# Pooled attention and a feed-forward layer on one core: half of the first loads issued by ScalarE, and a quarter of h copied out of its bank before g is made from it

## Chip, cores and metric

The kernel runs on one core of a Trainium2 chip. The metric is the device time of one execution in microseconds (us). Before the change three runs took 940.62, 941.49 and 943.90 us, so the median is 941.49 us. One further execution was recorded by the hardware profiler; it took 947.1 us.

## The reference

Keys and values are averaged over groups of 8 positions, so each of 8 batches and 8 heads has 576 queries but only 72 keys. The attention's result is laid out as 4608 tokens of 512 numbers and goes through a feed-forward layer of width 2048.

```python
batch, n_heads, seq, head_dim = (8, 8, 576, 64)
k_p = k.reshape(B, H, Sp, 8, D).mean(axis=3)
v_p = v.reshape(B, H, Sp, 8, D).mean(axis=3)
scores = scale * np.matmul(q, k_p.transpose(0, 1, 3, 2))
scores = scores - np.max(scores, axis=-1, keepdims=True)
attn = np.exp(scores)
attn = attn / (np.sum(attn, axis=-1, keepdims=True) + 1e-09)
attn_out = np.matmul(attn, v_p)
x = attn_out.transpose(0, 2, 1, 3).reshape(B * S, H * D)   # 4608 x 512
h = x @ w_in                                               # 512 x 2048
g = h * (1.0 / (1.0 + np.exp(-1.702 * h)))
out = g @ w_out                                            # 2048 x 512
```

## The kernel before

**Work.** All numbers are fp32. Every matrix operand of the feed-forward layer is kept as a rounded high part and a rest, and a product is three matmuls (high by high, rest by high, high by rest). Tokens go in chunks of 512. Chunk c is the first 512 tokens of batch c; chunk 8 gathers the 64 tokens that are left over in each batch. Chunks 0 and 1 are done by `dense`. While chunk 0 runs, the weights are still being loaded and decoded (`fetch_weights`, `decode`). From chunk 2 on, h is made pair by pair (`pair`): pair p of a chunk is two blocks of 128 columns of h by two halves of 256 tokens, that is four quarters, and these four quarters come from seven products instead of eight, with sums of weights that `fold` has stored in DRAM (`wd`) and that `fetch_pair` loads again for each chunk (`ws`, and `shared` for the fourth, half-sized part). During a chunk's eight pairs, the attention of the next batch is worked in between (`sum_keys`, `scores`, `sum_values`, `weigh`). The output products of pair p (`outputs`, tiles `o`) are placed among the products of pair p+1.

**A pair.** Two PSUM banks, `ha` and `hb`, hold running sums; all pairs and the dense chunks together have two buffers of this kind, so the next pair's `ha` is the last pair's `ha` buffer again, and its first product waits until that is read to the end. Four products go to `ha` (by the names of the weights: 11, s2, s3, 22), three to `hb` (12, s1, s4). After the first three products into `ha` the running sum is copied to a place in SBUF (`keep`, L1442); sums from `hb` are added to these places (`plus`, L1449). From a place, ScalarE makes g twice (`gelu`: L1466 the rounded high part `ghall`, L1474 the full value into the place), and DVE or POOL makes the rest `glall` (L1481). The fourth quarter is read by both activations straight from `ha`: `gelu(1, 0, 3, ha)`.

**Order.** A planner (`Plan`) holds every piece of work as a task with an engine, a modelled duration, a due time and buffers, plays it through once, and the instructions are written in the order in which tasks begin in that play. Each engine then works through its list strictly in this order. Some tasks may go to either of two engines (copies to ACT or DVE, rests to POOL or DVE); the play decides. The table `SHIFTS` moves due times by kind of task. While the first batch is not there yet, the list of PE is filled up with matmuls whose result nobody reads (`warm`, L1590); how many is fixed when the program is written.

**Loads.** All loads are issued on SP's queue, in list order, and a load into a reused buffer holds up the queue until that buffer is free. `fetch_main` (L464) loads a half of K or V of a batch in two DMAs of 256 KB, one to partitions 0 to 63 and one to 64 to 127. `fetch_last` and `fetch_tail` load the last keys (`tl`), which give `tred`, `tbd` and `vt`. `fetch_q_tile` (L1530, first batch only) loads 128 queries of all heads. `first_batch` sets the order of the first loads.

Of the kernel before, what the change touches and what calls it, by code (L numbers as in the profile page):

```python
# [256 lines left out]
def attention_moe_kernel(ctx: ExitStack, tc: tile.TileContext, q, k, v, w_in, w_out, out):  # L257


    nc = tc.nc  # L260
# [39 lines left out]
    def buf(pool, shape, dtype, tag, name, bufs=None, fifo=False):  # L300
        n = bufs or {"xpool": 2, "moe": 2, "ps_o": 4, "ps_h": 2, "ps_a": 2}.get(pool.name, 1)
        ring = rings.setdefault((pool.name, tag), Ring(n, fifo))
        kw = {"bufs": bufs} if bufs else {}
        return Buf(ring, lambda: pool.tile(shape, dtype, tag=tag, name=name, **kw), name)

    def dma(nbytes, emit, reads=(), writes=(), due=None, run=2048):

        us = nbytes / 1e3 / (340.0 if run >= 1024 else 190.0 if run >= 256 else 80.0)
        return plan.add("DMA", us, emit, reads, writes, due)
# [18 lines left out]
    def pe(ns, emit, reads, writes, due=None, also=(), mode="f32"):  # L328
# [8 lines left out]
        out=mask4[0:96], in_=ident[0:96].rearrange("p (r h e) -> p h r e", r=4, h=4), axis=AX.XY, op=ALU.add  # L337
# [3 lines left out]
        out=mask4[96:128, 0:2],  # L341
        in_=ident[96:128].rearrange("p (r a e) -> p a r e", r=8, a=2),
# [8 lines left out]
        out=mask, in_=ident.rearrange("p (r h e) -> p h r e", r=4, h=4), axis=AX.XY, op=ALU.add  # L351
# [3 lines left out]
        out=member, in_=ident.rearrange("p (r g e) -> p g r e", r=2, g=POOL), axis=AX.XY, op=ALU.add  # L355
# [72 lines left out]
    def x_op(c, name):  # L428
        if c not in x_ops:
            at = quarters([P, 2, CHUNK], F32R, f"x{c}")  # L430
            at += [home(2 * i, [P, 2, 512], F32R, f"xs{c}_{i}") for i in X_PLACES[(c - FROM) % 2]]
            x_ops[c] = {n: Op(b, n, lambda t: t) for n, b in zip(XOPS, at)}
        return x_ops[c][name]
# [7 lines left out]
    class Part:  # L441
# [8 lines left out]
        @property  # L450
        def ref(self):
            return (self.of, self.key)
# [4 lines left out]
    def fetch_main(b, u, src, t=None):  # L457

        if t is None:
            t = buf(load, [P, NP, 512], F32, "kv", f"kv{b}_{u}_{src is v}", fifo=True)  # L460
        for a in range(2):
            dma(
                KM * NP * 2048,
                lambda a=a: nc.sync.dma_start(  # L464
                    out=t()[a * KM : (a + 1) * KM],
                    in_=src[b, UH * u + a : UH * (u + 1) : 2, 0 : KM * POOL].rearrange(
                        "j (p w) d -> p j (w d)", w=POOL
                    ),
                ),
                writes=[ref(t)],  # L470
            )
        return t
# [929 lines left out]
    def pair(c, p, due, then):  # L1402


        nm = f"{c}_{p}"
        places = [c_slot(f"{nm}_{i}") for i in range(4)]

        def part(i):
            return places[i][0]()

        def at(i):
            return places[i][0]

        w = fetched[c, p]
        ha = buf(ps_h, [P, 512], F32, "h", f"ha{nm}")
        hb = buf(ps_h, [P, 512], F32, "h", f"hb{nm}")
        step = (ROUND - 10.0) / NPAIR / 10.6

        def product(at, wn, xn, bank, half, start):
            wb, wv = w[wn]  # L1420
            xo = x_op(c, xn)

            def emit():
                o = bank()[:, half * 256 : half * 256 + 256]
                terms = [(r, k, jj) for jj in range(2) for r, k in ((0, 0), (1, 0), (0, 1))]
                for n, (r, k, jj) in enumerate(terms):
                    nc.tensor.matmul(  # L1427
                        o,
                        lhsT=wv()[:, r, jj],
                        rhs=xo(k, jj),  # L1430
                        start=start and n == 0,
                        stop=n == len(terms) - 1,

                        skip_group_check=not start,
                    )

            plan.due = due + at * step
            pe(6 * 120, emit, [wb, *xo.refs(0), *xo.refs(1)], [bank], mode="f32r")

        def keep(i, bank):  # L1440
            plan.due = due - EAGER
            t = copy(256, lambda copy: copy(out=part(i), in_=bank()[:, 0:256]), [bank], [at(i)])  # L1442
            hold(t, places[i][1])

        def plus(i, half):
            plan.due = due - EAGER
            t = dve(
                256,
                lambda: nc.vector.tensor_tensor(  # L1449
                    out=part(i), in0=part(i), in1=hb()[:, half * 256 : half * 256 + 256], op=ALU.add  # L1450
                ),
                [hb],
                [at(i)],
            )
            hold(t, places[i][1])

        def gelu(f, th, i, bank=None):

            plan.due = due - EAGER
            gh, w1 = g_slot(f"{nm}_{f}{th}", "gh")  # L1460
            gl, w2 = g_slot(f"{nm}_{f}{th}", "gl")
            src = (lambda: bank()[:, 0:256]) if bank else (lambda: part(i))
            reads = [bank] if bank else [at(i)]
            t = act(
                256,
                lambda: nc.scalar.activation(out=gh(), in_=src(), func=AF.Gelu_apprx_sigmoid),  # L1466
                reads,
                [gh],
                table="gelu",
            )  # L1470
            hold(t, w1)
            act(
                256,
                lambda: nc.scalar.activation(out=part(i), in_=src(), func=AF.Gelu_apprx_sigmoid),  # L1474
                reads,
                [at(i)],
                table="gelu",
            )

            def rest(engine):  # L1480
                engine.tensor_tensor(out=gl(), in0=part(i), in1=gh().bitcast(F32), op=ALU.subtract)  # L1481

            if c == B:
                t = dve(256, lambda: rest(nc.vector), [at(i), gh], [gl], port=True)
            else:
                t = pool(256, lambda: rest(nc.gpsimd), [at(i), gh], [gl], other=lambda: rest(nc.vector))
            hold(t, w2, places[i][1])
            return gh, gl


        product(0, "11", "11", ha, 0, True)
        keep(0, ha)
        product(0.7, "12", "21", hb, 1, True)
        then(0, 2.0, 1.4, 2)
        product(2.8, "s2", "t2", ha, 0, False)
        keep(1, ha)
        product(3.5, "s1", "t1", hb, 0, True)
        plus(0, 1)
        got = {(0, 0): gelu(0, 0, 0)}
        then(2, 4.2, 0.7, 1)  # L1500
        product(4.9, "s3", "t3", ha, 0, False)
        keep(2, ha)
        plus(2, 0)
        then(3, 5.6, 0.7, 2)
        product(7.0, "22", "t4", ha, 0, False)
        got[1, 0] = gelu(1, 0, 3, ha)
        got[1, 1] = gelu(1, 1, 2)
        then(5, 7.7, 0.7, 3)
        product(9.8, "s4", "22", hb, 0, False)
        plus(1, 0)  # L1510
        got[0, 1] = gelu(0, 1, 1)
        return got
# [3 lines left out]
    def first_batch():  # L1516
        m = Batch()
        kv = quarters([P, NP, 512], F32, "kv0")
        m.k, m.v = kv[:NU], kv[NU:]
        m.tl = home(2 * NF - 4, [P, 512], F32, "tl0")  # L1520
        whole = []
        tiles = PIECES[0][1] + PIECES[1][1]
        places = [home(2 * NF - 1 - i, [P, 2, H, D], F32, f"q0_{i}") for i in range(3)]

        def fetch_q_tile(i):
            s0, ns = tiles[i]
            part = Part(places[i // 2], i % 2, lambda t: t[:ns, i % 2])
            dma(
                ns * H * D * 4,
                lambda: nc.sync.dma_start(out=part(), in_=q[0, :, s0 : s0 + ns].rearrange("h s d -> s h d")),  # L1530
                writes=[ref(part)],
                run=256,
            )
            whole.append(part)

        todo = {
            "k0": lambda: fetch_main(0, 0, k, m.k[0]),
            "k1": lambda: fetch_main(0, 1, k, m.k[1]),
            "v0": lambda: fetch_main(0, 0, v, m.v[0]),
            "v1": lambda: fetch_main(0, 1, v, m.v[1]),  # L1540
            "t": lambda: fetch_last(0, m.tl),
            "w": lambda: fetch_weights(len(raws)),
            "q": lambda: fetch_q_tile(len(whole)),
        }
        for n, what in enumerate("k0 k1 t q q v0 v1 w w w w w q q q w w".split()):
            plan.due = -100.0 + n
            todo[what]()
        return m, whole[:2], whole[2:]
# [92 lines left out]
    for c in range(FROM, B + 1):  # L1641
        acc = {}
        for p in range(NPAIR):
# [3 lines left out]
            got = pair(c, p, due, then)  # L1647
# [42 lines left out]
```

## Time and profile before

| | |
|---|---|
| median of three runs | 941.49 us (940.62 to 943.90) |
| the profiled execution | 947.1 us, of which 945.3 us are the span from the first to the last instruction |
| mean granted clock of PE | 0.996 |
| ACT and DVE in the stretch 540 to 640 us (one chunk with attention) | 64.31 and 76.49 us busy |
| ACT and DVE in the stretch 740 to 840 us (no attention beside it) | 44.17 and 40.46 us busy |
| last matmul, and last instruction | matmuls end near 940.3 us, then copies and stores follow |

A row of a timeline gives the start in us, the duration in us, the engine (PE matmul, PEld weight load, DVE, ACT, POOL; a trailing q marks the queue in which an engine issues DMAs), the line, the operation, output and inputs, and in brackets how long the engine had been idle before, and who ended the wait. A row of the list of waits gives the engine and line that waited, the engine and line waited for, the sum in us, how many times, and the longest. PEclk is the clock that PE was granted, as a share of full speed.

### The profile page before, as it was taken

What the parts mean: (1) busy time and instruction counts of PE and PEld (TensorE: products, weight loads), DVE (VectorE), ACT (ScalarE), POOL (GpSimd) and SP (SyncE); (2) the same over time, 40 slices, a digit from 0 to 9 for tenths busy, and PEclk for the clock granted to TensorE, in tenths of its full rate; (3) what the DMA queues carried; (4) which work ended last, traced back from release to release, by engine and by line L of the source; (5) the groups of instructions that cost most, each with busy time, mean ns of one, the idle gap of its engine ahead of it and who ended that gap; (6) DMA issues with size and microseconds to landing.
All of it is one profiled execution on the core that took longest, in us unless ns stands there. A gap on an engine that the chain in (4) does not pass through costs nothing.

```text
span 945.3 us, 16367 instructions
## 1 busy us (share of the span) xinstructions
PE 928.4 (98%) x5709; PEld 818.4 (87%) x5709; DVE 658.3 (70%) x1318; ACT 540.2 (57%) x1187; POOL 318.9 (34%) x307
## 2 busy tenths in 40 slices
PE   9999999999999999999999999999999999999997
PEld 8889888888788888889898988897888988899986
DVE  4987888885788787887588867886688643333332
ACT  3787765345437764767476746683578553334332
POOL 0755861778542233214221332124132350000000
PEclk9999999999999999999999999999899999999999
DMA  9993424436646478746983688358754665556541
GB/s 256 378 369 112 135 53 121 132 125 217 198 122 191 156 227 239 215 151 181 261 242 123 193 250 249 124 183 205 228 181 145 193 218 182 174 171 227 175 135 44
DMA packets 145266, 176.72 MB, mean 187 GB/s; under 512 B 85664, under 2 KB 96928, under 8 KB 145184
## 3 DMA queue, kind: packets, MB, share of 16 engines
q1 hardware_dynamic: 140336, 166.89, 58.6%
q10 hardware_dynamic: 4848, 8.78, 2.7%
q8 instruction: 45, 0.74, 0.3%
q14 instruction: 37, 0.30, 0.1%
HBM read 150.47 MB, written 25.17 MB: 186 GB/s over the span
## 4 chain that ended last, share of the span: by engine, by line
PE 80%; DMA 7%; DVE 6%; ACT 3%; issue 2%; SPq 1%; POOL 0%; ACTq 0%; DVEq 0%; POOLq 0%
PE ha L1427 14%; PE hb L1427 11%; PE o L1627 9%; PE o L1629 9%; PE o L1628 9%; PE sps L743 4%; DMA kv_False<-in_k_dram 3%; PE h L1223 3%; PE h L1225 3%; PE h L1224 3%; PE o L1265 3%; PE o L1266 2%; PE o L1267 2%; DMA qr<-in_q_dram 2%; PE warm L1590 2%
## 5 line engine op out<-in xcount | busy, mean ns | idle before, releaser
L1627 PE MATMUL o<-w,ghall 128*128 128x512 f32 x448 | 177.2, 396 | 0.0
L1629 PE MATMUL o<-w,glall 128*128 128x512 f32 x448 | 176.8, 395 | 0.0
L1628 PE MATMUL o<-w,ghall 128*128 128x512 f32 x448 | 176.2, 393 | 0.0
L1481 POOL TENSOR_TENSOR glall<-shared,ghall 128x256 fp32r<-128x256 f32 x88 | 73.1, 832 | 225.5 <-ACT shared L1474 176.2
L1427 PE MATMUL hb<-x,ws 128*128 128x256 f32 x672 | 99.8, 286 | 1.6 <-DVE shared L1449 1.2
L1629 PEld LDWEIGHTS o<-w,glall 128*128 128x128 f32 x448 | 84.4, 188 | 19.0 <-POOL glall L1481 0.3
L1427 PEld LDWEIGHTS ha<-xs,ws 128*128 128x128 f32 x672 | 93.3, 189 | 7.7 <-issue 0.8
L1427 PE MATMUL ha<-xs,ws 128*128 128x256 f32 x672 | 99.0, 283 | 0.0
L1427 PEld LDWEIGHTS hb<-x,ws 128*128 128x128 f32 x672 | 91.1, 190 | 7.2 <-DVE shared L1449 2.6
L1627 PEld LDWEIGHTS o<-w,ghall 128*128 128x128 f32 x448 | 84.9, 190 | 9.1 <-issue 0.8
L1628 PEld LDWEIGHTS o<-w,ghall 128*128 128x128 f32 x448 | 84.4, 188 | 8.4
L1449 DVE TENSOR_TENSOR shared<-shared,hb 128x256 f32<-128x256 f32 x112 | 46.5, 415 | 55.5 <-PE hb L1427 45.6
L1466 ACT ACTIVATE ghall<-shared 128x256 fp32r<-128x256 f32 x112 | 46.8, 418 | 65.3 <-DVE shared L1449 46.4
L1481 POOL TENSOR_TENSOR glall<-gall,ghall 128x256 fp32r<-128x256 f32 x42 | 33.0, 785 | 96.4 <-ACT gall L1474 71.9
L1481 DVE TENSOR_TENSOR glall<-shared,ghall 128x256 fp32r<-128x256 f32 x62 | 31.3, 506 | 48.9 <-ACT shared L1474 47.4
L1223 PE MATMUL h<-x,w 128*128 128x256 f32 (+1 forms) x192 | 63.1, 329 | 0.0
L1224 PE MATMUL h<-x,w 128*128 128x256 f32 (+1 forms) x192 | 61.1, 318 | 0.0
L1225 PE MATMUL h<-x,w 128*128 128x256 f32 (+1 forms) x192 | 61.1, 318 | 0.0
L1442 ACT COPY shared<-ha 128x256 f32<-128x256 f32 x60 | 22.3, 371 | 57.0 <-PE ha L1427 56.9
L1427 PE MATMUL ha<-x,ws 128*128 128x256 f32 x336 | 51.1, 289 | 2.3 <-ACT shared L1474 1.6
L1253 POOL TENSOR_TENSOR gl<-g,gh 128x512 fp32r<-128x512 f32 x27 | 39.9, 1479 | 39.0 <-ACT gh L1245 29.4
L1427 PEld LDWEIGHTS ha<-x,shared 128*128 128x128 f32 x336 | 47.0, 188 | 7.1 <-ACT shared L1442 2.9
(177 smaller groups left out, 2173.4 us busy)
## 6 DMA issues: line engine op xcount, KB each, us to landing
ws<-wd SPq DMA_DIRECT2D x168, 512.0 KB
shared<-wd SPq DMA_DIRECT2D x56, 256.0 KB
out_dram<-osb ACTq DMA_DIRECT2D x32, 256.0 KB
wd<-stage SPq DMA_DIRECT2D x16, 512.0 KB
raw<-in_moe_w_in_dram SPq DMA_DIRECT2D x15, 512.0 KB
raw<-in_moe_w_out_dram SPq DMA_DIRECT2D x15, 512.0 KB
kv_False<-in_k_dram SPq DMA_DIRECT2D x28, 256.0 KB
kv_True<-in_v_dram SPq DMA_DIRECT2D x28, 256.0 KB
```

Source lines behind the costliest of these rows:

```text
L743: nc.tensor.matmul(ps()[:ns, t * PW : (t + 1) * PW], lhsT=qt()[:, s0 - o0 : s0 - o0 + ns], rhs=m.k2()[:, jj], start=True, stop=True,)
L1223: nc.tensor.matmul(o, lhsT=w[:, 0, j], rhs=xs[:, 0], start=j == 0, stop=False)
L1224: nc.tensor.matmul(o, lhsT=w[:, 1, j], rhs=xs[:, 0], start=False, stop=False)
L1225: nc.tensor.matmul(o, lhsT=w[:, 0, j], rhs=xs[:, 1], start=False, stop=j == NJ - 1)
L1253: engine.tensor_tensor(out=gl(), in0=g(), in1=gh().bitcast(F32), op=ALU.subtract)
L1427: nc.tensor.matmul(o, lhsT=wv()[:, r, jj], rhs=xo(k, jj), start=start and n == 0, stop=n == len(terms) - 1,  skip_group_check=not start,)
L1449: lambda: nc.vector.tensor_tensor(out=part(i), in0=part(i), in1=hb()[:, half * 256 : half * 256 + 256], op=ALU.add),
L1466: lambda: nc.scalar.activation(out=gh(), in_=src(), func=AF.Gelu_apprx_sigmoid),
L1481: engine.tensor_tensor(out=gl(), in0=part(i), in1=gh().bitcast(F32), op=ALU.subtract)
L1627: nc.tensor.matmul(o(), lhsT=gh()[:, tok], rhs=w()[:, 0], start=start, stop=False)
L1628: nc.tensor.matmul(o(), lhsT=gh()[:, tok], rhs=w()[:, 1], start=False, stop=False)
L1629: nc.tensor.matmul(o(), lhsT=gl()[:, tok], rhs=w()[:, 0], start=False, stop=stop)
```

## The change

Three edits. In `fetch_main`, the DMA to the upper 64 partitions is issued on ScalarE's queue when the batch is 0. In `fetch_q_tile`, the first two tiles of q are issued there too. In `pair`, the fourth quarter is copied from `ha` to its place by `keep(3, ha)`, and its g is made from that copy.

```diff
--- before.py
+++ after.py
@@ fetch_main
-                lambda a=a: nc.sync.dma_start(
+                lambda a=a: (nc.scalar if a and b == 0 else nc.sync).dma_start(
                     out=t()[a * KM : (a + 1) * KM],
@@ pair
         product(7.0, "22", "t4", ha, 0, False)
-        got[1, 0] = gelu(1, 0, 3, ha)
+        keep(3, ha)
+        got[1, 0] = gelu(1, 0, 3)
         got[1, 1] = gelu(1, 1, 2)
@@ first_batch, fetch_q_tile
-                lambda: nc.sync.dma_start(out=part(), in_=q[0, :, s0 : s0 + ns].rearrange("h s d -> s h d")),
+                lambda: (nc.scalar if i < 2 else nc.sync).dma_start(
+                    out=part(), in_=q[0, :, s0 : s0 + ns].rearrange("h s d -> s h d")
+                ),
```

The new task in `pair` makes the planner's play come out differently, so lists are reordered from chunk 2 on; up to there PE's, DVE's and POOL's lists are the same as before, and so are, but for the six DMAs, those of ACT and SP. PE has 5382 instructions in both. There are 56 copies more (L1442: 168 before, 224 after; the 56 are all on ACT, which has 148 instead of 90, while DVE has 76 instead of 78), and 20 rests (L1481) go from POOL (130, now 110) to DVE (94, now 114). Three places are shown. Lines of the changed kernel stand one to four higher.

**ACT at the program's start.** `kv_137` and `kv_140` are the two halves of K, `kv_181` and `kv_189` those of V, all of batch 0. Before:

```order
L683 ACT_TABLE_LOAD
L683 CAST vt_197<-tbd_187 96x512
L722 COPY qt_0_0_208<-qps_0_0_194 128x256
L722 COPY qt_0_1_216<-qps_0_1_199 128x256
L650 ACTIVATE k_218<-kps_0_202 128x288
```

After:

```order
L465 DMA kv_137<-in_k_dram 64x2x512
L465 DMA kv_140<-in_k_dram 64x2x512
L1532 DMA q_0_167<-in_q_dram 128x8x64 x2
L465 DMA kv_181<-in_v_dram 64x2x512
L684 ACT_TABLE_LOAD
L684 CAST vt_197<-tbd_187 96x512
L465 DMA kv_189<-in_v_dram 64x2x512
L723 COPY qt_0_0_208<-qps_0_0_194 128x256
```

Five DMAs now stand ahead of ACT's first work, and the sixth, the upper half of V's second half, stands behind the cast of `vt`, which needs `tbd`.

**SP at the last batch boundary** (batch 7's keys are loaded while a chunk goes over to the next; `ws_0_1` is part 1 of the next chunk's pair 0, `shared` its part 3; `tl_1` are the last keys of the second half). Before:

```order
L1018 DMA left_dram<-left_1_7363 512x1x64
L1360 DMA ws_0_0_7483<-wd_0_97 128x1024
L464 DMA kv_1_False<-in_k_dram 64x2x512
L513 DMA qr_0_1_7451<-in_q_dram 32x8x32 x3
L1360 DMA ws_0_1_7524<-wd_1_98 128x1024
L513 DMA qr_0_2_7536<-in_q_dram 32x8x32 x3
L1360 DMA shared_2591<-wd_3_100 128x512
L480 DMA tl_1_7561<-in_v_dram 32x1x512 x3
L480 DMA tl_1_7561<-in_k_dram 32x1x512
```

After:

```order
L1361 DMA ws_0_0_7499<-wd_0_97 128x1024
L1019 DMA left_dram<-left_1_7375 512x1x64
L465 DMA kv_1_False<-in_k_dram 64x2x512 x2
L481 DMA tl_1_7548<-in_v_dram 32x1x512
L1361 DMA ws_0_1_7556<-wd_1_98 128x1024
L481 DMA tl_1_7548<-in_v_dram 32x1x512 x2
L481 DMA tl_1_7548<-in_k_dram 32x1x512
L514 DMA qr_0_2_7579<-in_q_dram 32x8x32 x2
L1361 DMA shared_2591<-wd_3_100 128x512
```

The last DMA of `tl_1` stood behind `shared` and now stands ahead of it, behind `ws_0_1`. At the two boundaries ahead of this one it stood ahead of `ws_0_1` before and stands behind it after; at all three, both DMAs of `kv_1` now stand behind `ws_0_0`.

**The hand-over of `ha` from pair to pair, on ACT and on PE.** ACT around pair 1 of chunk 5 (`main` and `tail` are parts of the next batch's attention), before:

```order
L867 COPY main_0_6791<-sc_0_6619 32x2x4x32 x2
L1466 ACTIVATE ghall_3179<-ha_1_6693 128x256
L1474 ACTIVATE shared_3069<-ha_1_6693 128x256
L857 COPY tail_0_6788<-sc_0_6619 32x2x32
L867 COPY main_0_6791<-sc_0_6619 32x2x4x32
```

and after:

```order
L868 COPY main_0_6816<-sc_0_6643 32x2x4x32 x2
L1443 COPY shared_3069<-ha_1_6718 128x256
L1467 ACTIVATE ghall_3179<-shared_3069 128x256
L1475 ACTIVATE shared_3069<-shared_3069 128x256
L1467 ACTIVATE ghall_3195<-gall 128x256
```

The copy stands where the first of the two activations stood. PE between pair 4 and pair 5 of the same chunk, before:

```order
L1427 MATMUL ha_4_7138<-x_6385,shared_2591 128x256 x6
L1427 MATMUL hb_4_7151<-xs_14_6257,ws_4_2_6986 128x256 x6
L1627 MATMUL o_0_6703<-w_8_1155,ghall_3179 128x512
L1628 MATMUL o_0_6703<-w_8_1155,ghall_3179 128x512
L1629 MATMUL o_0_6703<-w_8_1155,glall_3189 128x512
L1427 MATMUL ha_5_7271<-x_5813,ws_5_0_7017 128x256 x6
```

and after:

```order
L1631 MATMUL o_0_6728<-w_8_1155,ghall_3179 128x512
L1632 MATMUL o_0_6728<-w_8_1155,ghall_3179 128x512
L1633 MATMUL o_0_6728<-w_8_1155,glall_3189 128x512
L1428 MATMUL ha_4_7166<-x_6414,shared_2591 128x256 x6
L1428 MATMUL hb_4_7178<-xs_14_6277,ws_4_2_7011 128x256 x6
L1428 MATMUL ha_5_7298<-x_5832,ws_5_0_7044 128x256 x6
```

One output product has moved ahead, so between the last product into `ha` and the next pair's first one stands only one product of six matmuls. Counted over the whole list, 18 of the 55 hand-overs stand this close after the change (eight of them in chunk 7), and none before.

## The prediction

> **What bounds the kernel.** I read the page's totals first.
>
> ```profile
> span 945.3 us, 16367 instructions
> PE 928.4 (98%) x5709; PEld 818.4 (87%) x5709; DVE 658.3 (70%) x1318; ACT 540.2 (57%) x1187; POOL 318.9 (34%) x307
> ```
>
> PE is busy in 98% of the span. Its work does not change here, so the change can move the time only through the 945.3 − 928.4 = 16.9 us in which PE stands still (some 5 of them behind the last matmul, as the table ahead shows), and through the clock at which PE works. The list of PE's waits says what ended the idle time:
>
> ```profile
> PE ha L1427 <- ACT shared L1442: 2.5, 1, 2.5
> PE ha L1427 <- ACT shared L1474: 1.6, 4, 0.6
> PE warm L1590 <- POOL ident masks.py:199: 1.4, 1, 1.4
> PE ha L1427 <- ACT gall L1474: 0.5, 1, 0.5
> ```
>
> One wait of 2.5 us stands out. Five others, 2.1 us in all, are for ScalarE's second activation (L1474), the one that reads `ha` and that the change replaces. Next the windows: us, busy time of PE, PEld, DVE, ACT and POOL, PEclk, DMA share, GB/s.
>
> ```profile
> 0.00:20.00 20.00, 18.57 (x135) 17.49 (x136) 8.15 (x22) 5.29 (x11) 1.22 (x7) 1.00 0.94 259
> 20.00:45.00 25.00, 23.45 (x189) 21.43 (x190) 23.53 (x42) 19.30 (x39) 17.01 (x15) 1.00 1.02 357
> 540.00:640.00 100.00, 98.84 (x624) 87.92 (x623) 76.49 (x167) 64.31 (x149) 28.79 (x33) 1.00 0.68 200
> 657.00:664.00 7.00, 4.51 (x27) 3.65 (x26) 3.50 (x7) 2.03 (x5) 0.00 (x0) 1.00 0.86 228
> 664.00:671.00 7.00, 7.00 (x29) 5.82 (x28) 3.29 (x4) 2.77 (x8) 1.46 (x2) 0.51 0.64 208
> ```
>
> Behind the long wait, PE works for 7 us at a clock of 0.51, which loses 7.00 × 0.49 = 3.43 us. So one place of this execution costs 2.49 + 3.43 = 5.9 us.
>
> The timeline says where the wait comes from:
>
> ```profile
> 646.94 0.34 SPq L1360 DMA_DIRECT2D ws<-wd  x1
> ...
> 651.49 0.34 SPq L1360 DMA_DIRECT2D shared<-wd  x1
> 651.93 2.09 SPq L480 DMA_DIRECT2D tl<-in_v_dram  x3
> 654.07 0.63 SPq L480 DMA_DIRECT2D tl<-in_k_dram  x1
> ...
> 659.52 1.06 DVE L603 TENSOR_REDUCE tred<-tl 128x64 f32<-128x512 f32 x1 [5.35 <-DMA tl<-in_k_dram]
> ...
> 661.28 0.62 ACT L683 CAST vt<-tbd 96x512 fp32r<-96x512 f32 x1 [5.28 <-DVE tbd L613]
> ...
> 662.98 0.98 PE L1427 MATMUL ha<-x,shared 128*128 128x256 f32 x6 [2.49 <-ACT shared L1442]
> ```
>
> SP issues the last keys (`tl`) only behind the weights `shared`, at 654.07. They land 5.45 us later; DVE has stood 5.35 us at `tred` by then, ACT 5.28 us at the cast of `vt`, and the copy that PE needs is queued behind that cast. The engine named in the wait, ACT, is not slow: a DMA was issued late.
>
> **The change, term by term.** *1. The last keys move ahead of `shared`.* In the new list all of `tl_1` is issued ahead of `shared`, the K part behind `ws_0_1`, which goes out at 646.94. With that DMA's 0.34 us, two more parts at 2.09 / 3 = 0.70 each, K is issued near 648.7, and 5.45 us on it is there at 654.1. PE needed `tred` to begin 662.98 − 659.52 = 3.46 us ahead of its own start, thus by 660.48 − 3.46 = 657.0. So 2.9 us are to spare: −2.49 us, and with it the half clock, −3.43 us. Next late there would be the cast of `vt` in its new place on DVE; it has the same 2.9 us.
>
> By the Trainium skill (TensorE: Matmul & The Clock Gate, section "What's actually happening"), the clock falls only after an idle window of about 3.4 us that runs freely. Here it fell after 2.49 us, so the trace does not agree in length. By that rule the 3.43 us would not be this wait's, and only 2.49 would go.
>
> *2. The hand-over of `ha`.* The longest of the five small waits, on ACT:
>
> ```profile
> 587.61 0.82 ACT L867 COPY main<-sc 32x256 f32<-32x256 f32 x2
> 588.46 0.38 ACT L1466 ACTIVATE ghall<-ha 128x256 fp32r<-128x256 f32 x1
> 588.74 0.38 ACT L1474 ACTIVATE shared<-ha 128x256 f32<-128x256 f32 x1
> ```
>
> and on PE, whose first product of the next pair is the last row:
>
> ```profile
> 586.29 0.88 PE L1427 MATMUL ha<-x,shared 128*128 128x256 f32 x6
> 587.01 0.89 PE L1427 MATMUL hb<-xs,ws 128*128 128x256 f32 x6
> ...
> 589.17 0.98 PE L1427 MATMUL ha<-x,ws 128*128 128x256 f32 x6 [0.57 <-ACT shared L1474]
> ```
>
> What a copy costs in place of the two activations, and what a rest costs on DVE, I take from the groups by shape (count | busy us, mean ns | idle before):
>
> ```profile
> L1481 DVE TENSOR_TENSOR glall<-shared,ghall 128x256 fp32r<-128x256 f32 x62 | 31.3, 506 | 48.9 <-ACT shared L1474 47.4 <-issue 1.4
> ...
> L1442 ACT COPY shared<-ha 128x256 f32<-128x256 f32 x60 | 22.3, 371 | 57.0 <-PE ha L1427 56.9
> L1442 DVE COPY shared<-ha 128x256 f32<-128x256 f32 x52 | 21.9, 420 | 8.2 <-PE ha L1427 7.8
> ```
>
> Before, `ha` is read until 588.74 + 0.38 = 589.12. A copy of 0.37 us that begins at 588.46 ends at 588.83, 0.29 us sooner. Five waits give at most 5 × 0.29 = 1.45; I take −1.4.
>
> *3. The load of the copies.* 56 × 0.371 = 20.8 us more on ACT, and 20 rests of 0.506, 10.1 us, more on DVE, over seven chunks of about 100 us: 3.0 and 1.4 us in 100. The stretch 540:640 has 64.31 us of ACT and 76.49 of DVE in 100, so neither comes near full. I take 0; the cover is PE's own products, and without it the price would be the 20.8 us.
>
> *4. Tight hand-overs.* The new order leaves one product, in place of two or an output block, between the last product into `ha` and the next pair's first, 18 times. From the last product to the moment when ACT can read the bank, the timeline shows:
>
> ```profile
> 794.60 0.86 PE L1427 MATMUL ha<-x,shared 128*128 128x256 f32 x6
> ...
> 795.50 0.39 ACT L1466 ACTIVATE ghall<-ha 128x256 fp32r<-128x256 f32 x1 [0.76 <-PE ha L1427]
> ```
>
> ACT can read `ha` 0.90 us after the last product began (795.50 − 794.60), and the copy is over 0.37 later, at 1.27 (1.32 on DVE, 0.42). PE wants the bank after that product and one more, each 0.72 by the rows 586.29 and 587.01 above (587.01 − 586.29), thus at 1.44. It fits by 0.12 to 0.17 us if the engine is free at that moment. Ends: 0, and 18 × 0.37 = 6.7 where each copy finds one other piece ahead of it. ACT is 44 to 64% busy, but the planner has put the copy where it expects the engine free; I take +0.5, near the row of the free engine.
>
> *5. The head.* Six of the first DMAs go out on ACT's queue.
>
> ```profile
> 7.22 2.73 SPq L464 DMA_DIRECT2D kv<-in_v_dram  x4
> ...
> 11.65 0.62 ACT L683 CAST vt<-tbd 96x512 fp32r<-96x512 f32 x1 [9.63 <-DVE tbd L590]
> ...
> 13.62 2.05 PE L532 MATMUL red_v<-kv,ident 128*128 128x128 f32 x16
> ...
> 16.71 1.95 PE L532 MATMUL red_v<-kv,ident 128*128 128x128 f32 x16
> ```
>
> PE is filled there with a fixed number of `warm` matmuls, in both lists the same, and its list of waits names no load in the first 20 us (18.57 busy, and 1.4 us is the start). So loads that land sooner bring nothing: 0. Later ones cost. V's last upper half was issued by 7.22 + 2.73 = 9.95; now it stands on ACT behind the cast that ends at 12.27, and is issued by 12.27 + 2.73 / 4 = 12.95. How long it takes to land has an upper end in V's first half, issued by 8.59 and read at 13.62 without a wait: at most 5.0 us, which makes 17.95, 1.2 behind the 16.71 at which PE wants it; with the 5.45 us of `tl` it would be 1.7. The lower end is a landing by 16.71, in 3.8 us, and nothing. Both figures are ends by which a load had landed, so I take a quarter, +0.3. A gain has an end as well: all of PE's idle time in the stretch 20:45, 25.00 − 23.45 = 1.5 us, if later loads were the cause.
>
> DMA engines are 0.94 busy in the first 20 us with one queue. The Trainium skill (DMA: Bandwidth & Descriptors, section "Issuing engines are not separate DMA queues") says that DMAs issued from several engines share the same 16 and interleave, which saves issue time alone; it gives the same 0, and the row agrees.
>
> **The sum.** Profiled execution: 947.1 − 2.49 − 3.43 − 1.4 + 0.5 + 0.3 = 940.6. The median of the runs is 5.6 lower than the profiled execution, nearly as much as the two parts of term 1 (5.92), so it must be decided whether the timed runs had them. Their spread helps: 943.90 − 941.49 = 2.4 and 943.90 − 940.62 = 3.3, about one stretch at half clock. I choose: the wait follows from SP's order and is in every run, the half clock in one of three. Then 941.49 − 2.49 − 1.4 + 0.5 + 0.3 = **938.4**.
>
> **Rivals.**
>
> *The runs had neither.* 941.49 − 0.6 = 940.9. For it: the 5.6 us. Against it: the late issue is in the list.
>
> *The runs had both* (chance of their median): 938.4 − 3.43 = 935.0.
>
> *Waits come back elsewhere.* A third of the tight hand-overs with 0.37 us, and one new wait of 1 us: 940.9 of the case above, or 938.4 + 6 × 0.37 + 1 = 941.6. For it: 0.12 us of slack on DVE.
>
> *Slower: late keys at three boundaries.* The order in front shows that `tl_1` stands ahead of `ws_0_1` at two boundaries before and behind it now; at all three `kv_1` stands behind `ws_0_0`. One boundary before:
>
> ```profile
> 547.41 0.63 SPq L480 DMA_DIRECT2D tl<-in_k_dram  x1
> ...
> 549.97 0.34 SPq L1360 DMA_DIRECT2D ws<-wd  x1
> ...
> 553.82 1.08 DVE L603 TENSOR_REDUCE tred<-tl 128x64 f32<-128x512 f32 x1
> ...
> 561.48 0.75 PE L1427 MATMUL ha<-x,shared 128*128 128x256 f32 x5
> ```
>
> PE wants its product at 561.48, so `tred` must begin by 561.48 − 3.46 = 558.0, and its load, at 5.45 us, must be issued by 552.6. Behind `ws` it goes out near 550.3 or, with two other parts of `tl`, 551.7: 0.9 to 2.3 us to spare. Where SP is held up by as much (a buffer that is not free), each boundary stands for up to 2.49: 938.4 + 3 × 2.49 = 945.9, and with 3.43 each of half clock 956. Against it: 5.35 us of the old wait were needed to cost 2.49. One boundary alone gives 940.9 to 944.3.
>
> *The head gains.* 938.4 − 1.8 = 936.6, if later loads and not the fixed list set its end; PE's list of waits speaks against it.
>
> **Chances.** Forecast 0.35 (of it 0.05 lands above 938.7), both 0.13, head 0.02, neither 0.22, waits elsewhere 0.09, late keys 0.19. A measurement of this kernel can tell about 0.3%, 2.8 us, from no change: 938.7 to 944.3. Faster is 0.30 + 0.13 + 0.02 = 0.45, the same 0.05 + 0.22 + 0.09 = 0.36, slower 0.19. The range reaches down to 934.0 (the case of both, less 1 for the head) and up to 945.0 (the forecast with 6.7 for term 4 is 944.6); of late keys most is left out. The forecast's own range is 936.5 to 940.5, which spans both signs with the case "neither".
>
> **What would show it.** Right: no wait of PE of over 1 us near 660, PEclk 1.00 in the windows behind it, `tl` issued ahead of 651 there, and no wait of DVE over 2 us at `tred`; the waits for L1474 gone, those for the copy under 0.2 us each; `red_v`'s second half with under 1 us. Wrong: waits for `tred` or the copy at the boundaries near 455, 552 or 660, many waits of 0.3 us at `ha`, or a profile that is 6 us shorter while the runs' median stays, which would say that the median never had the wait.

## The result and the profile after

| | before | after |
|---|---|---|
| median | 941.22 us (940.62 to 943.90, 4 runs) | 952.17 us (950.85 to 954.72, 4 runs) |
| ratio, with its 95% interval | | 1.0121 (1.0097 to 1.0144) |
| profiled execution | 947.1 us, span 945.3 | 951.37 us, span 949.5 |

The kernel became slower by 10.95 us, 1.2%. The totals of the page after:

```profile
span 949.5 us, 16436 instructions
PE 928.4 (98%) x5709; PEld 817.6 (86%) x5709; DVE 673.4 (71%) x1356; ACT 557.9 (59%) x1221; POOL 313.8 (33%) x291
```

PE's busy time is 928.4 us as before, so its 16.9 us of standing still have become 21.1. PE's waits after the change (engine and line that waited, what for: sum, times, longest; lines stand one to four higher):

```profile
PE sps L744 <- ACT k L651: 5.2, 1, 5.2
PE ha L1428 <- ACT shared L1443: 2.5, 4, 1.1
...
PE ha L1428 <- DVE shared L1443: 0.7, 2, 0.5
...
PE ha L1428 <- DVE gall L1450: 0.6, 1, 0.6
```

The 2.5 us wait for `ha<-x,shared` near 660 us is gone, but a wait of 5.2 us stands in the program's head, where none was: the first scores wait for `k`, which ScalarE makes. Everything behind the head comes some 8 us later now, so the old place near 660 has moved to about 671. The windows of the two places (us, busy time of PE, PEld, DVE, ACT and POOL, PEclk, DMA share, GB/s):

```profile
0.00:20.00 20.00, 14.45 (x98) 13.08 (x98) 4.49 (x14) 1.90 (x2) 0.70 (x6) 0.96 0.96 268
20.00:45.00 25.00, 21.66 (x167) 20.39 (x168) 20.09 (x33) 16.64 (x34) 11.11 (x11) 0.89 1.04 362
18.40:25.70 7.30, 3.82 (x17) 3.44 (x18) 2.08 (x5) 2.46 (x7) 0.00 (x0) 0.53 1.03 271
657.00:664.00 7.00, 7.00 (x49) 6.38 (x48) 6.96 (x9) 4.03 (x10) 4.60 (x5) 1.00 0.87 216
664.00:671.00 7.00, 7.00 (x43) 6.04 (x41) 4.55 (x10) 3.35 (x9) 0.74 (x1) 1.00 0.88 242
671.00:678.00 7.00, 7.00 (x47) 6.33 (x46) 3.58 (x6) 2.85 (x8) 0.74 (x1) 1.00 0.92 307
```

From 657 to 678 us PE works without a break at full clock, as forecast. In the first 45 us it is busy 14.45 + 21.66 = 36.1 us, against 18.57 + 23.45 = 42.0 before, 5.9 less; and in the second window its mean clock is 0.89 where it was 1.00, which loses another 21.66 × 0.11 = 2.4 (by the narrower row from 18.4 to 25.7, where the slow clock lies, 3.82 × 0.47 = 1.8). That makes PE 7.7 to 8.3 us late when the head is over. The same instruction of DVE's list, which waits for scores that PE makes, is 114.47 − 106.14 = 8.3 us late. Before:

```profile
106.14 0.42 DVE L768 TENSOR_REDUCE nm<-sps 128x4 f32<-128x288 f32 x1
```

After:

```profile
114.47 0.42 DVE L769 TENSOR_REDUCE nm<-sps 128x4 f32<-128x288 f32 x1
```

The other 2.7 us of the 10.95 are not assigned to a place by this profile. The timeline of the head shows what ScalarE did meanwhile (ACTq and SPq are the queues in which an engine issues DMAs):

```profile
10.41 0.33 SPq L1090 DMA_DIRECT2D raw<-in_moe_w_out_dram  x1
...
12.47 0.62 ACT L684 CAST vt<-tbd 96x512 fp32r<-96x512 f32 x1 [3.71 <-DVE tbd L591]
...
20.04 0.60 ACTq L465 DMA_DIRECT2D kv<-in_v_dram  x1
20.68 0.65 ACT L723 COPY qt<-qps 128x256 f32<-128x256 f32 x2 [7.60 <-DMA raw<-in_moe_w_out_dram]
21.22 0.73 ACT L651 ACTIVATE k<-kps 128x288 f32<-128x288 f32 x2
...
21.70 2.29 PE L744 MATMUL sps<-k,qt 128*128 128x144 f32 x8 [5.21 <-ACT k L651]
...
24.60 2.35 PE L533 MATMUL red_v<-kv,ident 128*128 128x128 f32 x16 [0.18 <-DMA q<-in_q_dram]
```

From 13.09, when the cast ends, to 20.04 ScalarE does nothing. Next in its list is the sixth of the moved DMAs, the upper half of V's second half, and it is not issued until 20.04. The copies of q and the activations that make `k` are queued behind it, and PE's first scores behind those. The releaser that the profile names is a load of weights from `in_moe_w_out`; by the compiled lists it is the one that SP issued at 10.41. Each row of these lists names what it waits for; these are rows of the changed kernel, first of ACT, then of SP:

```
L684 CAST vt_197<-tbd_187 96x512 [waits DVE]
L465 DMA kv_189<-in_v_dram 64x2x512 [waits DMAHW6]
L723 COPY qt_0_0_208<-qps_0_0_194 128x256 [waits PE]

L1090 DMA raw_220<-in_moe_w_in_dram 128x4x256 [waits DMAHW3]
L1090 DMA raw_232<-in_moe_w_out_dram 128x1024 [waits DMAHW4]
L1090 DMA raw_260<-in_moe_w_in_dram 128x4x256 [waits DMAHW5]
L1090 DMA raw_268<-in_moe_w_out_dram 128x1024 [waits DMAHW6]
...
L1090 DMA raw_370<-in_moe_w_out_dram 128x1024 [waits DMAHW5]
L1090 DMA raw_382<-in_moe_w_in_dram 128x4x256 [waits DMAHW7]
```

The names DMAHW0 to DMAHW7 are eight counters that DMAs raise when they land. DMAs of both queues take them in turn, in one common order, and in these lists a DMA waits until the counter's user before it, the eighth DMA before itself, has landed. SP's rows show where the sixth DMA stands in that order: between `raw_370` with counter 5 and `raw_382` with counter 7, the twelfth DMA behind its own other half. Its forerunner on counter 6 is `raw_268`, the fourth load of weights, issued at 10.41.

### The profile page after: what moved, and what is told of

The parts are those of the page before. It is cut to its first block, busy times and chain, and to the rows that moved or that the text cites. A ratio compares the mean times of both kernels' runs of the same rounds, so it can differ in the third digit from the quotient of the medians.

```text
span 949.5 us, 16436 instructions
## 1 busy us (share of the span) xinstructions
PE 928.4 (98%) x5709; PEld 817.6 (86%) x5709; DVE 673.4 (71%) x1356; ACT 557.9 (59%) x1221; POOL 313.8 (33%) x291
## 4 chain that ended last, share of the span: by engine, by line
PE 87%; DMA 6%; DVE 3%; ACT 2%; SPq 1%; issue 1%; ACTq 0%; POOL 0%; DVEq 0%; POOLq 0%
PE ha L1428 16%; PE hb L1428 11%; PE o L1631 10%; PE o L1633 10%; PE o L1632 10%; PE sps L744 4%; PE h L1224 3%; PE h L1226 3%; PE h L1225 3%; PE o L1266 3%; PE o L1267 3%; PE o L1268 3%; DMA qr<-in_q_dram 2%; PE pav L965 1%; DMA kv<-in_v_dram 1%; PE warm L1594 1%
## 5 line engine op out<-in xcount | busy, mean ns | idle before, releaser
L1482 POOL TENSOR_TENSOR glall<-shared,ghall 128x256 fp32r<-128x256 f32 x72 | 60.5, 841 | 202.6 <-ACT shared L1475 159.2
L1467 ACT ACTIVATE ghall<-shared 128x256 fp32r<-128x256 f32 x150 | 62.4, 416 | 60.3 <-DVE shared L1450 42.7
L1482 DVE TENSOR_TENSOR glall<-shared,ghall 128x256 fp32r<-128x256 f32 x78 | 40.1, 514 | 52.5 <-ACT shared L1475 52.3
L1443 ACT COPY shared<-ha 128x256 f32<-128x256 f32 x100 | 37.0, 370 | 65.5 <-PE ha L1428 62.6
L1475 ACT ACTIVATE shared<-shared 128x256 f32<-128x256 f32 x150 | 62.5, 418 | 4.6
L744 PE MATMUL sps<-k,qt 128*128 128x144 f32 (+1 forms) x320 | 54.1, 301 | 5.3 <-ACT k L651 5.2
L744 PEld LDWEIGHTS sps<-k,qt 128*128 128x128 f32 (+1 forms) x320 | 42.4, 182 | 14.7 <-ACT k L651 5.4
```

The source lines that it names most:

```text
L744: nc.tensor.matmul(ps()[:ns, t * PW : (t + 1) * PW], lhsT=qt()[:, s0 - o0 : s0 - o0 + ns], rhs=m.k2()[:, jj], start=True, stop=True,)
```

## Experiments

**Which edit costs the time?** Four runs, on one chip; each ratio, here and further below, is against runs of the kernel before on the same chip beside it. The first is the kernel before, once more.

> The kernel before, unchanged, profiled once more. Question: does the 2.5 us wait of PE near 660 us, with the stretch at a granted clock of 0.51 behind it, come back? Theory A (it belongs to the one execution that was profiled, 947.1 us; the timed runs near 941.2 hadn't both): time 941 +- 1, the wait near 660 under 1 us or without the half clock. Rival B (it is in every run): a profile of 945 to 947 us with both again, and runs near 941 only because a profile adds some 5 us.

Measured: 942.59 us (939.36 to 946.87, 10 runs), against 941.24 (938.20 to 946.35, 29 runs) for the runs of the same kernel beside it, ratio 1.0015 (0.9996 to 1.0035). The profiled execution, 946.87 us, is the longest of the ten, and its longest wait stands elsewhere. The row of that wait, then the windows around it, and then the old place:

```profile
PE hb L1427 <- DVE gall L1449: 2.7, 2, 2.3
```

```profile
457.00:460.50 3.50, 0.97 (x6) 0.77 (x6) 3.49 (x6) 1.38 (x4) 0.51 (x1) 1.00 0.63 194
460.50:464.00 3.50, 3.48 (x13) 3.19 (x14) 3.40 (x7) 1.10 (x3) 0.83 (x2) 0.51 0.84 199
```

```profile
658.91 0.63 SPq L480 DMA_DIRECT2D tl<-in_k_dram  x1
...
662.81 1.08 DVE L603 TENSOR_REDUCE tred<-tl 128x64 f32<-128x512 f32 x1 [3.82 <-DMA tl<-in_k_dram]
...
666.28 0.98 PE L1427 MATMUL ha<-x,shared 128*128 128x256 f32 x6 [0.99 <-ACT shared L1442]
```

The wait of 2.3 us and the stretch at 0.51 are now at 457 us, another boundary of chunks, and at the old place PE waits 0.99 us. The place of the long wait changes with the execution, which speaks against rival B; but the profiled time is as high as rival B said. A third profile, further below, settles it.

The DMA edits alone, on the kernel before:

```diff
-                lambda a=a: nc.sync.dma_start(
+                lambda a=a: (nc.scalar if a and b == 0 else nc.sync).dma_start(
...
-                lambda: nc.sync.dma_start(out=part(), ...
+                lambda: (nc.scalar if i < 2 else nc.sync).dma_start(out=part(), ...
```

> The kernel before with the six DMAs on ScalarE's queue, without the copy: the lists from chunk 2 on are those of before. Theory A (ScalarE's list stands at the sixth DMA from 13.1 to 20.0 us, since that DMA waits for the landing of weights issued at 10.4 us; PE waits 5.2 us for k and then works 6.8 us at half clock): 941.2 + 8.3 = 949.5, with the same 5 us wait of PE at sps. Rival B (the copy and the new order are the cause, the head's loss is made good before the end): 941 to 943.

Measured: 950.98 us (949.82 to 953.63), ratio 1.0107 (1.0077 to 1.0136). PE's longest wait is the one of the changed kernel:

```profile
PE sps L743 <- ACT k L650: 5.3, 1, 5.3
```

So these edits alone bring nearly the whole loss, 9.7 us against the 8.3 that theory A had, and theory A holds.

The copy alone, all loads on SP's queue:

```diff
-        got[1, 0] = gelu(1, 0, 3, ha)
+        keep(3, ha)
+        got[1, 0] = gelu(1, 0, 3)
```

> The kernel before with the copy of the fourth quarter, all loads on SP's queue. Theory A (8.3 of the change's 10.9 us are the head's): 952.2 - 8.3 = 943.9, 2.7 above before, from waits of PE at ha (3.8 us in the changed kernel's profile, 2.1 before). Rival B (as predicted, without the head): 938.1 to 940.6. Rival C (the copies alone slow it): above 948.

Measured: 942.89 us (940.90 to 946.97, 12 runs), ratio 1.0017 (1.0001 to 1.0033). That is 1.0 below theory A's figure and above the forecast's 938.1 to 940.6; a second copy of the kernel before came out at 1.0015. The copies and the new order neither won nor lost what these runs can tell. In this kernel's profile the last keys do go out ahead of `shared` (at 649.92 and 651.81 us), as the prediction wanted.

The changed kernel with one DMA back:

```diff
-                lambda a=a: (nc.scalar if a and b == 0 else nc.sync).dma_start(
+                lambda a=a: (nc.scalar if a and b == 0 and not (u and src is v) else nc.sync).dma_start(
```

> The changed kernel with one of the six DMAs, the upper half of V's second half, back on SP's queue. Theory A (that one DMA holds up ScalarE): the head's loss is gone, 943.9, and no wait of PE over 1 us before 36 us. Rival B (the loss is from loads that land later because two queues share the DMA engines): still over 948, with waits of PE for loads or for k in the first 25 us.

Measured: 942.56 us (940.27 to 946.12, 12 runs), ratio 1.0013 (0.9996 to 1.0030). Its timeline:

```profile
13.07 0.63 ACT L723 COPY qt<-qps 128x256 f32<-128x256 f32 x2
...
16.41 1.15 PE L744 MATMUL sps<-k,qt 128*128 128x144 f32 x8
17.61 1.95 PE L533 MATMUL red_v<-kv,ident 128*128 128x128 f32 x16
```

With five of the six DMAs still on ScalarE's queue, the copies of q follow the cast at once, the first scores begin at 16.41 in place of 21.70, and 952.17 − 942.56 = 9.6 us are won back. One DMA made the loss.

**Is it the counter, the place in the list, or the second queue?** Three kernels leave the sixth DMA on ScalarE's queue and change whom it follows. First it goes ahead of the cast, by moving its task behind the other half's in the order that is written out:

```diff
+    heads = [t for t in plan.tasks if t.engine == "DMA"][10:12]
+    order.remove(heads[1])
+    order.insert(order.index(heads[0]), heads[1])
     with tc.manual_schedule():
```

> The changed kernel, all six DMAs still on ScalarE's queue, but the sixth (upper half of V's second half) put ahead of the cast of vt in ScalarE's list. By its list it now shares its completion counter with the other half of the same tile's loads or an early load, not with the weights issued at 10.4 us. Theory A (the DMA instruction waits until the earlier user of its counter has landed, and all of ScalarE's list waits with it): it is issued by 8 to 9 us, no wait of PE over 1 us before 25 us, no half clock, 942.6 as with that DMA on SP. Rival B (any second queue for V costs, through shared DMA engines or ScalarE's time for issuing): over 947.

Measured: 942.75 us (941.60 to 948.94, 12 runs), ratio 1.0019 (1.0000 to 1.0038). In the compiled list it now waits for DMAHW2, whose user before it is the upper half of K's second half, the second DMA that ScalarE issues.

```profile
4.38 3.44 ACTq L465 DMA_DIRECT2D kv<-in_v_dram  x2
...
12.77 0.64 ACT L723 COPY qt<-qps 128x256 f32<-128x256 f32 x2
...
16.10 1.15 PE L744 MATMUL sps<-k,qt 128*128 128x144 f32 x8
17.30 1.95 PE L533 MATMUL red_v<-kv,ident 128*128 128x128 f32 x16
```

Both upper halves of V are issued by 7.82, and the loss is gone with all six DMAs on the second queue. Rival B falls.

Then it goes behind the activations that make `k`; there its counter, by the list, was last used by the last q tile:

```diff
+    head = [t for t in plan.tasks if t.engine == "DMA"][11]
+    order.remove(head)
+    order.insert(order.index([t for t in order if t.kind.startswith("ACT k0")][1]) + 1, head)
     with tc.manual_schedule():
```

> The changed kernel with the sixth DMA put behind the two activations that make k in ScalarE's list. By its list it now shares its counter with the last q tile, which SP issues near 20 us. Theory A: k and the first scores come in time (no 5 us wait at sps), but the DMA goes out only when that q tile has landed, after 21 us, so V's second half is late at red_v: PE waits 5 to 10 us there, and the time is 948 to 956. Rival B (the DMA waits for nothing and only stood badly ahead of k): it goes out near 15 us and the time is within 2 us of 943.

Measured: 958.41 us (957.40 to 960.70, 4 runs), ratio 1.0187 (1.0162 to 1.0213).

```profile
13.83 7.44 SPq L1532 DMA_DIRECT2D q<-in_q_dram  x3
...
16.48 1.15 PE L744 MATMUL sps<-k,qt 128*128 128x144 f32 x8
...
23.66 0.60 ACTq L465 DMA_DIRECT2D kv<-in_v_dram  x1
...
24.36 0.37 ACT L723 COPY qt<-qps 128x256 f32<-128x256 f32 x1 [9.25 <-DMA q<-in_q_dram]
...
31.63 0.58 PE L533 MATMUL red_v<-kv,ident 128*128 128x128 f32 x1 [13.79 <-DMA kv<-in_v_dram]
```

The scores come in time, ScalarE stands until the q tile has landed, 2.4 us after SP issued the last one (23.66 − 21.27), and PE waits for V instead, 13.8 us. The mechanism is as expected; the size is not: theory A had a wait of 5 to 10 us and 948 to 956 in all, since it counted nothing for V's own way, which took 31.63 − 24.26 = 7.4 us beside the loads that SP issued.

Last, the DMA stays at its place behind the cast, and the DMAs ahead of it change places, so that its forerunner is the first load of weights:

```diff
+    d = [t for t in plan.tasks if t.engine == "DMA"]
+    three, last = d[17:20], d[12]
+    for t in three:
+        order.remove(t)
+        order.insert(order.index(last), t)
     with tc.manual_schedule():
```

> The changed kernel with the last three q tiles issued by SP ahead of the first weights instead of behind five of them. The sixth DMA stands at the same place in ScalarE's list as in the changed kernel; by its list it still shares a counter with the eighth DMA before it, which is now the very first of the weights instead of the fourth. Theory A (it waits for that one to land): it goes out when the first weights are there, some 3 to 6 us earlier than 20.0, so the wait of PE at sps shrinks to 0 to 3 us. Rival B (it waits because of its place behind the cast, or for the fourth weights, or for room in a queue): 20 us and a wait of 5 us again.

Measured: 955.09 us (951.96 to 955.38, 4 runs), ratio 1.0162 (1.0137 to 1.0187).

```profile
13.51 0.62 SPq L1090 DMA_DIRECT2D raw<-in_moe_w_in_dram  x1
...
18.21 0.60 ACTq L465 DMA_DIRECT2D kv<-in_v_dram  x1
18.85 0.65 ACT L723 COPY qt<-qps 128x256 f32<-128x256 f32 x2 [5.74 <-DMA raw<-in_moe_w_in_dram]
...
19.86 1.98 PE L744 MATMUL sps<-k,qt 128*128 128x144 f32 x8 [3.35 <-ACT k L651]
...
26.81 3.54 PE L533 MATMUL red_v<-kv,ident 128*128 128x128 f32 x15 [4.54 <-DMA kv<-in_v_dram]
```

The releaser is now a load of `in_moe_w_in`, no longer one of `in_moe_w_out`, as the list says. At an unchanged place the DMA goes out 4.7 us after the issue of its new forerunner. That is 1.8 us sooner than in the changed kernel and not the 3 to 6 expected, because SP spent 8.12 to 13.47 on issuing the three q tiles. The wait at `sps` shrank to 3.35 us, a little more than the 0 to 3 expected, and the time did not fall below the changed kernel's, since PE now also waits 4.54 us for V. The same list without the hold:

> The run before with the sixth DMA on SP's queue: what the new order of loads costs by itself, with no DMA behind work of ScalarE. Theory: within 2 us of 942.6, no wait of PE over 1.5 us in the first 25 us; the difference to the run before is then the hold alone, 0 to 6 us.

Measured: 945.61 us (943.22 to 949.50, 5 runs), ratio 1.0066 (1.0037 to 1.0095): the order of loads costs more by itself than the 2 us allowed. In its profile PE waits 2.0 us near 31 us for `main`, where it waited 1.1 before, and the mean clock from 20 to 45 us is 0.93; that the later weights are behind this is not shown. Against the run before, the hold is worth 955.09 − 945.61 = 9.5 us, also more than the 6 expected: in the profile of the run before, PE waits 3.35 us for `k` and 4.54 for V, besides the clock.

**Do the other edits win anything?** Only the q tiles on the second queue:

```diff
-                lambda a=a: (nc.scalar if a and b == 0 else nc.sync).dma_start(
+                lambda a=a: nc.sync.dma_start(
```

> The changed kernel with only the two q tiles on ScalarE's queue, K and V all on SP's. Theory A: no DMA stands behind work of ScalarE, so nothing is lost and, since PE's list is filled with a fixed number of matmuls there, nothing is won: 942 to 943, the first long product as in the kernel before. Rival (q earlier shortens the head): below 940.

Measured: 942.86 us (940.67 to 945.46, 12 runs), ratio 1.0021 (1.0007 to 1.0036). Nothing is won; in the profile, a wait stands at K's first use that the kernel before did not have:

```profile
PE red_k L533 <- DMA kv<-in_k_dram: 1.3, 1, 1.3
```

K's and V's halves on the second queue win nothing either: the two kernels above with five and with six DMAs there and no hold measured 1.0013 and 1.0019.

**Was the 5.9 us wait in the runs at all?** A third profile of the kernel before:

> The kernel before, a third profile. Question: is the wait at the boundary of chunks a matter of the single execution? Theory: waits of PE of 1 to 3 us and stretches of half clock stand at other boundaries than 660 us or are missing, and the profiled time follows them (941 without, 945 to 947 with); the median of the timed runs stays 941 to 943. Rival: 2.5 us at 660 again.

Measured: 939.34 us (938.03 to 942.02, 10 runs), ratio 0.9988 (0.9973 to 1.0004); the profiled execution took 939.5 us, as much as its median, so being profiled does not add 5 us. At the place of the old wait:

```profile
652.43 0.63 SPq L480 DMA_DIRECT2D tl<-in_k_dram  x1
655.95 1.06 DVE L603 TENSOR_REDUCE tred<-tl 128x64 f32<-128x512 f32 x1 [3.43 <-DMA tl<-in_k_dram]
...
659.40 0.97 PE L1427 MATMUL ha<-x,shared 128*128 128x256 f32 x6 [0.57 <-ACT shared L1442]
```

The order is the same, `tl` behind `shared`, which SP issued at 649.85. The load took 655.95 − 652.43 = 3.5 us to land instead of 5.45, 1.9 less, and PE's wait is 0.57 instead of 2.49, also 1.9 less. No half clock follows. The second profile lies between the two: 662.81 − 658.91 = 3.9 us to land, and a wait of 0.99. So the late issue belongs to the order and is in all three profiles, but the size of the wait follows the landing time, and the 2.5 us with the 3.4 us behind it stand in one of the three alone.

## Why the prediction was wrong

The forecast was 938.4 us with a range of 934.0 to 945.0; the runs gave 952.17.

- **The step that failed is term 5, the head**, at the words "is issued by 12.95". The prediction saw that V's last upper half now stands behind the cast, and asked only how long it takes to land. It took for granted that a DMA goes out when the engine reaches it. The DMA waited 7 us for its counter, until 20.04, and with it waited all that is queued behind it on ScalarE: two copies and the activations that make `k`. The first scores, not `red_v`, were the work that PE had to wait for: 5.21 us, against 0.18 at `red_v`'s second half. The term was +0.3 with an end of 1.7; the edits alone measured 950.98 − 941.24 = 9.7 us, and taking the one DMA back won 9.6. In the profile 5.2 of it are the wait for `k`, and 1.8 to 2.4 the half clock that came with it.
- **Term 1 was right as a mechanism and missing from the median.** In the changed kernel's profile the last keys go out ahead of `shared`, and the wait near 660 us and its half clock are gone, though this load took 6.64 us to land in place of 5.45:

```profile
658.78 0.63 SPq L481 DMA_DIRECT2D tl<-in_k_dram  x1
...
661.26 0.34 SPq L1361 DMA_DIRECT2D shared<-wd  x1
...
665.42 1.09 DVE L604 TENSOR_REDUCE tred<-tl 128x64 f32<-128x512 f32 x1 [0.69 <-DMA tl<-in_k_dram]
```

But most runs near 941 us can hardly have had the 5.9 us to lose: the three profiles have waits of 2.49, 0.99 and 0.57 us there, and the copy-only kernel, which also issues the last keys ahead of `shared`, is no faster. For this term that is the rival "the runs had neither". The prediction reasoned that a wait which follows from the order of the list must be in every run; its size followed from a landing time that changes with the execution. The agreement of 947.1 − 941.49 = 5.6 with 2.49 + 3.43 was the better sign.
- **Terms 2 and 4, the hand-overs.** The waits for L1474 are gone, as forecast, but others for `ha` took their place: 2.5 + 0.7 + 0.6 = 3.8 us after, 2.1 before besides the wait of 2.5. The sum of the two terms was −0.9; the profiles say +1.7. The third profile of before has 1.9 us of waits at `ha`, the second 3.3, so this is no more than profiles of one kernel differ. The sign "those for the copy under 0.2 us each" was not met: ScalarE's copy is waited for four times, up to 1.1 us. Whether the tight hand-overs cost 1 us stays open: four kernels with the copy and without the hold (the copy alone, one DMA back, the sixth ahead of the cast, q alone) measured 1.0013 to 1.0021, and two copies of the kernel before 0.9988 and 1.0015.
- **Term 3, the load of the copies at nothing, was right.** ACT's busy time rises by 557.9 − 540.2 = 17.7 us, and DVE's by 15.1, without a price that shows.
- **The rival that ended slower** was put at late keys at three boundaries. It did not happen: at the three boundaries DVE waits for the last keys 0.69 us at most, and PE does not wait there at all. The slower case had another cause, at a place where the prediction had seen a risk, but priced it by the landing of one load alone.

The hold of ScalarE's list is shown by the compiled lists and by the five kernels that move it or take it away. Where 1.3 to 1.9 us of its cost lie stays open: taking it away won 9.6 us in the runs, and the profile shows 7.7 to 8.3. None of the versions tried beats the kernel before by what can be measured.

## What to carry to other kernels

A DMA that was issued on a computing engine's queue brought its wait into that engine's list here: before moving one, read what it waits for, its counter's earlier user included, and what stands behind it there. Put such a DMA ahead of all work that it could hold up (here 942.75 against 952.17 us, ratios 1.0019 and 1.0121, for the same six DMAs), or leave it on the queue that does nothing else. And take a wait found in one profile off the median only when a second profile has it at the same size; the first hint is how far that profile's own time lies above the runs.

## What was not expected of the hardware

- A load's time to land differs much. The 256 KB of V's upper half took 7.4 us with the DMA issued at 23.66 and 26.81 − 18.81 = 8.0 us with the one issued at 18.21, in a stretch in which the DMA engines were busy all the time (share 1.06 from 20 to 45 us in the latter run). The last keys took 5.45, 3.9 and 3.5 us in three executions of one kernel. Which loads beside them account for it was not separated.
- The clock fell to 0.51 behind a wait of 2.49 us and behind one of 2.30, about 1 us of work and one of 0.53; in the wait of 5.21 us it fell some 2 us after the wait had begun (PEclk 0.96 over the first 20 us, and 0.53 from 18.4 to 25.7). It did not fall behind 1.46 us at `ha` in the run with one DMA back, whose mean granted clock is 0.999. With the DMA edits alone it fell behind 1.46 and 0.53 us with about 1 us of work between them. How long the slow stretch lasts differs: 6.8 us behind the wait of 2.49, 3.4 us behind that of 2.30.
